# Attention with a Mish layer block on one core: the clamp of ten of 14 first-layer units moved from ScalarE to GpSimd, and GpSimd's work cut into more pieces

## The chip, the cores and the metric

The kernel runs on one core of a Trainium2 chip. The core has a matrix engine (TensorE; PE in the profile, with its weight loads as PEld), VectorE (DVE), ScalarE (ACT), GpSimd (POOL) and SyncE (SP), whose queue issues the DMAs. Each engine works through its own list of instructions in order and waits for the others by semaphores. The metric is the device time of one execution in microseconds, as the median of several runs. All times below are microseconds unless marked ns.

## The reference, cut to what matters

One transformer block in float32 on 2048 rows of 512: an adaptive layer norm, full softmax attention with 32 heads of 16, a gated residual, a second layer norm, and two dense layers (512 to 1792 to 512) with the Mish activation between them.

```python
h = _layernorm(x, axis=-1) * (1 + ca) + sa
x = x + ga * _A_ref(h, A_wqkv, A_wo)          # softmax(q k^T / 4) v, then wo
h = _layernorm(x, axis=-1) * (1 + cb) + sb
x = x + gb * _B_ref(h, B_w1, B_b1, B_w2)
...
def _B_ref(x, w1, b1, w2):
    h = jnp.einsum("bsd,df->bsf", x, w1) + b1
    sp = jnp.log1p(jnp.exp(-jnp.abs(h))) + jnp.where(h > 0, h, jnp.zeros_like(h))
    act = h * jnp.tanh(sp)
    return jnp.einsum("bsf,fd->bsd", act, w2)
```

The kernel uses another form of Mish: with e = exp(min(h, 10)) and u = e (e + 2), it is h u / (u + 2). One over (u + 2) is made as exp(-ln(u + 2)) on ScalarE and refined by one Newton step.

## The kernel before, in words

The rows are cut into four blocks of 512 queries (`NB`), the heads into eight groups of four (`G`); a pair of block and group is an iteration `n`, and an iteration has 16 steps, one for each chunk `kc` of 128 keys. `step(t)` writes out one step, and two half steps make a step (`h` counts half steps). In a step TensorE makes four score products for this iteration (`score`, line 505), each followed on ScalarE by an exponential out of PSUM (`pr`, line 508), four products for the row maxima of a later iteration (`max_tile`, line 468), each reduced by VectorE (line 470), and at the end the product of probabilities and values of two steps earlier (`pv`, line 523). The products of lines 468 and 505 go round a ring of six PSUM banks (`ring`), and a bank comes free when VectorE or ScalarE has read it.

Beside them TensorE is given parts of a queue of other units: projections and weight preparation at first, and from about a third of the time on the layer block of one block of 512 queries, three times (`block(qb, t0)`; the last block's is made in `tail()` after attention is through). Its order is written out by hand with `queue_up` and `queue_down`: an up unit `f` (0 to 13) makes 128 columns of the first layer, a down unit `(gi, i)` adds a group of up units into 128 rows of the second. The units' order is up 0 to 4; down (0,0), up 5, down (0,1), up 6, down (0,2), down (0,3), up 7, up 8; the same again with the next group and up 9 to 12; down (2,0), up 13, and the rest. So up 8 and up 12 follow another up unit directly, as do 1 to 4. A unit takes two or four steps of TensorE's spare slots, and when its last product is out, `fin(h)` is called, with `h` the half step that follows.

What an up unit does behind TensorE is `mish`, in stages that `fin` puts into later half steps with `at(h, f)`. `hooks[h]` is a list that `run_hooks(h)` runs in order, twice a step, and the position there decides where in each engine's list an instruction stands. The stages before:

- s1, at `h`: `hb` = product + bias (ScalarE, line 713; VectorE, line 711, where no maxima are left to make)
- s2, at `h + 1`: the clamp, `ee` = relu(10 - hb) (ScalarE, line 716)
- s2b, at `h + 2`: `ee` = exp(10 - ee), which is exp(min(hb, 10)) (ScalarE, line 719)
- s3, at `h + 3`: `ee` = (ee + 2) ee (VectorE, line 722), then `hb` = hb ee (GpSimd, line 723)
- s4, at `h + 4`: `rr` = ln(ee + 2) (ScalarE, line 726)
- s5, at `h + 6`: `rr` = exp(-rr) (ScalarE, line 729), then on GpSimd five operations in lines 735 to 739, the rounding of the result to `a_h` (line 93, `hi_copy`) and the rest `a_l` = hb - a_h (line 96, `lo_sub`)

A down unit ends with a copy of its bank by ScalarE (`yd`, line 864) and an addition by GpSimd (`y`, line 865). Each iteration ends with `evac(n)`: ScalarE copies the accumulated attention output out of PSUM (line 537), DMAs spread it and the row sums, and for each pair of groups `norm` multiplies by the reciprocals on GpSimd (`od`, line 566), rounds (line 93) and subtracts (line 96) at a half step set by line 570. The tiles `ee` and `rr` have two buffers, `hb` three, `qq` one.

In `tail()` the same stages run without attention, with `tail=True`; there VectorE does what GpSimd does in lines 723 and 735 to 739.

Of the kernel before, what the change touches and what calls it, by code (L numbers as in the profile page):

```python
# [18 lines left out]
def adaln_block(ctx: ExitStack, tc: tile.TileContext, x, wqkv, wo, w1, b1, w2, c, w_mod, out):  # L19
    nc = tc.nc  # L20
# [510 lines left out]
    def evac(n):  # L531
# [30 lines left out]
        if g % 2 == 1 or n == NIT - 2:  # L562
            r = slice(0, P if g % 2 else 64)

            def norm():
                nc.gpsimd.tensor_mul(od[r], od[r], rb[r])
                oh, ol = o_hl[qb]
                hi_copy("p", oh[r, g // 2, :], od[r])
                lo_sub("p", ol[r, g // 2, :], od[r], oh[r, g // 2, :])
            at(2 * t1 + (29 if g == 1 else 17 if hurry else 23), norm)  # L570
# [128 lines left out]
    def mish(f, acc, tail):  # L699
# [15 lines left out]
        def s2():  # L715
            nc.scalar.activation(ee, hb, AF.Relu, bias=hcap, scale=-1.0)

        def s2b():
            nc.scalar.activation(ee, ee, AF.Exp, bias=hcap, scale=-1.0)  # L719

        def s3():
            nc.vector.scalar_tensor_tensor(ee, ee, 2.0, ee, op0=ALU.add, op1=ALU.mult)  # L722
            (nc.vector if tail else nc.gpsimd).tensor_mul(hb, hb, ee)  # L723
# [4 lines left out]
        def s5():  # L728
# [5 lines left out]
            else:  # L734
                nc.gpsimd.tensor_scalar(ee, ee, 1.0, 2.0, op0=ALU.mult, op1=ALU.add)
                nc.gpsimd.tensor_mul(qq, ee, rr)  # L736
                nc.gpsimd.tensor_scalar(qq, qq, -1.0, 2.0, op0=ALU.mult, op1=ALU.add)
                nc.gpsimd.tensor_mul(rr, rr, qq)  # L738
                nc.gpsimd.tensor_mul(hb, hb, rr)
            hi_copy("v" if tail and f > FT - 4 else "p", a_h, hb)  # L740
            lo_sub("v" if tail and f > FT - 4 else "p", a_l, hb, a_h)

        return (a_h, a_l), (s1, s2, s2b, s3, s4, s5)
# [7 lines left out]
    HELD = 2  # L751
    state = [({}, {}, {}, {}) for _ in range(NB)]

    def block(qb, t0):
# [79 lines left out]
        def up_unit(f, tag):  # L834
# [3 lines left out]
            act[f], stages = mish(f, acc, False)  # L838

            def fin(h):  # L840
                stages[0](idle(h))
                for i, s in zip((1, 2, 3, 4, 6), stages[1:]):
                    at(h + i, s)
                done["a", f] = h + 6
# [44 lines left out]
        def queue_down(gi, i):  # L889
            queue(lambda l=groups[gi][-1]: done.get(("a", l), 4 * T) + 1, lambda tag: down_unit(gi, i, tag))  # L890
# [53 lines left out]
    def tail():  # L944
# [64 lines left out]
        for u in range(FT + LAG):  # L1009
# [7 lines left out]
            for d, ss in ((2, (4, 5)), (1, (2, 3)), (0, (0, 1))):  # L1017
                if 0 <= u - d < FT:
                    for q in ss:
                        stages[u - d][q]()  # L1020
# [301 lines left out]
```

## Time and profile before

| | us |
|---|---|
| median of three runs | 1742.61 |
| lowest and highest run | 1740.09, 1744.63 |
| profiled execution | 1738.89 |
| its span in the profile | 1737.1 |
| granted TensorE clock, mean share | 0.998 |

The three layer blocks lie between about 560 and 1625 of the span; from about 1570 on there are no maxima left to make, and attention ends at about 1625. How to read the lines: the page gives for each engine busy time, share of the span and number of instructions. A row of busy time in a stretch gives the stretch, its length, then for PE, PEld, DVE, ACT and POOL the busy time and number of instructions, the granted clock, the share of DMA time and GB/s. A row of a timeline gives start, duration, engine, source line, operation, output and input, and in brackets the idle time before it and what ended it. A row of a group ends with total busy time, mean ns of one, and idle time before.

### The profile page before, as it was taken

The page shows a single profiled execution, that of the slowest core. Times are in us where ns is not written, and L with a number is a line of the kernel's source. Part 1 is how long each engine was busy: PE and PEld are TensorE (multiplying, and loading weights), DVE is VectorE, ACT ScalarE, POOL GpSimd, SP SyncE. Part 2 cuts the span into 40 slices and gives each one's busy share as a digit, 9 for nine tenths or more (in the row PEclk, how much of TensorE's full clock was granted, in tenths as well). Part 3 has the DMA queues.
Part 4 walks back from the last instruction along what each step waited for, and adds up shares of the span by engine and source line. Part 5 has one row for each costly group of instructions (what it writes and reads, how often), then busy time and mean ns, then how long its engine had stood idle before and what let it go on. Part 6 is the DMA issues. An engine that isn't in the chain of part 4 may idle for free.

```text
span 1737.1 us, 33698 instructions
## 1 busy us (share of the span) xinstructions
PE 1702.3 (98%) x12396; PEld 963.9 (55%) x12396; DVE 1464.9 (84%) x2464; ACT 1349.4 (78%) x2581; POOL 729.0 (42%) x723
## 2 busy tenths in 40 slices
PE   7999999999999999999999999999999999999999
PEld 5755655555435555555555555555555555554587
DVE  6987888888898998989889898888898999892377
ACT  6257777777777898888877898888878988888474
POOL 5131124665303373444523374434423464444552
PEclk9999999999999999999999999999999999999999
DMA  7777467777762432524353533434252543423261
GB/s 251 187 254 189 114 172 202 234 235 223 218 184 52 136 96 77 136 77 121 89 137 87 162 97 88 139 90 124 71 156 73 152 102 103 115 79 130 85 230 61
DMA packets 113997, 240.08 MB, mean 138 GB/s; under 512 B 24048, under 2 KB 49648, under 8 KB 107784
## 3 DMA queue, kind: packets, MB, share of 16 engines
q1 hardware_dynamic: 113832, 237.92, 48.0%
q8 instruction: 98, 1.61, 0.4%
q14 instruction: 67, 0.55, 0.1%
HBM read 179.95 MB, written 51.44 MB: 133 GB/s over the span
## 4 chain that ended last, share of the span: by engine, by line
PE 80%; DMA 8%; DVE 4%; POOL 2%; ACT 2%; issue 2%; SPq 1%; POOLq 0%; ACTq 0%; DVEq 0%
PE bk L523 26%; PE ring L468 19%; PE ring L505 18%; PE bk L130 12%; PE ring L124 2%; DMA qscr<-ql 2%; DVE mx L470 2%; PE ring L1028 1%; DMA w1scr<-hl 1%; ACT pr L508 1%; PE bk L124 1%; DMA woscr<-hl 1%; DMA xt<-in_A_x 1%; DMA kscr<-ql 1%; DMA hl<-in_B_w 1%
## 5 line engine op out<-in xcount | busy, mean ns | idle before, releaser
L470 DVE TENSOR_REDUCE mx<-ring 128x1 f32<-128x512 f32 x2048 | 1274.0, 682 | 166.5 <-PE ring L468 134.7
L508 ACT ACTIVATE pr<-ring 128x512 f32<-128x512 f32 x2048 | 1083.3, 603 | 256.1 <-PE bk L130 161.4
L468 PE MATMUL ring<-ka,qa 64*128 64x512 f32 x2048 | 850.6, 429 | 0.9 <-DVE mx L470 0.4
L505 PE MATMUL ring<-qa,ka 64*128 64x512 f32 x2048 | 726.1, 398 | 7.0 <-ACT pr L508 5.8
L468 PEld LDWEIGHTS ring<-ka,qa 64*128 64x128 f32 x2048 | 366.4, 184 | 414.2 <-DVE mx L470 334.5
L523 PE MATMUL bk<-pr,vg 128*32 128x512 f32 x4096 | 546.3, 606 | 0.0
L505 PEld LDWEIGHTS ring<-qa,ka 64*128 64x128 f32 x2048 | 374.1, 185 | 88.3 <-ACT pr L508 34.4
L130 PE MATMUL bk<-h,w 64*128 64x512 f32 (+1 forms) x1080 | 279.0, 392 | 1.4 <-ACT pr L508 1.3
L130 PE MATMUL bk<-w,a_h 64*128 64x512 f32 x608 | 204.9, 416 | 1.4 <-ACT pr L508 1.2
L130 PEld LDWEIGHTS bk<-h,w 64*128 64x128 f32 x1080 | 178.5, 184 | 19.0 <-ACT pr L508 8.7
L723 POOL TENSOR_TENSOR hb<-hb,ee 128x512 f32<-128x512 f32 x42 | 54.0, 1286 | 293.9 <-DVE ee L722 293.9
L523 PEld LDWEIGHTS bk<-pr,vg 128*32 128x32 f32 x4096 | 81.6, 108 | 131.8 <-issue 126.0
L130 PE MATMUL bk<-w,a_l 64*128 64x512 f32 x304 | 119.4, 393 | 0.0
L130 PEld LDWEIGHTS bk<-w,a_h 64*128 64x128 f32 x608 | 100.9, 184 | 10.4 <-ACT pr L508 5.8
L865 POOL TENSOR_TENSOR y<-yd,y 128x512 f32<-128x512 f32 x48 | 62.0, 1295 | 80.4 <-ACT yd L864 80.2
L736 POOL TENSOR_TENSOR qq<-ee,rr 128x512 f32<-128x512 f32 x42 | 54.3, 1292 | 76.9 <-ACT rr L729 76.7
L130 PE MATMUL bk<-w,o_hl 64*128 64x512 f32 x288 | 81.5, 414 | 2.2 <-POOL o_hl L93 1.1
L96 POOL TENSOR_TENSOR a_l<-hb,a_h 128x512 fp32r<-128x512 f32 x53 | 72.3, 1363 | 4.4
L130 PEld LDWEIGHTS bk<-w,a_l 64*128 64x128 f32 x304 | 56.0, 184 | 3.0
L130 PE MATMUL bk<-h_h,wl 64*128 64x512 f32 x168 | 56.8, 419 | 0.0
L722 DVE SCALAR_TENSOR_TENSOR ee<-ee 128x512 f32<-128x512 f32 x56 | 41.4, 740 | 17.0 <-ACT ee L719 17.0
L738 POOL TENSOR_TENSOR rr<-rr,qq 128x512 f32<-128x512 f32 x42 | 54.1, 1287 | 3.5
(185 smaller groups left out, 1703.1 us busy)
## 6 DMA issues: line engine op xcount, KB each, us to landing
ka<-kscr SPq DMA_DIRECT2D x124, 384.0 KB
w<-w2scr SPq DMA_DIRECT2D x56, 512.0 KB
w<-w1scr SPq DMA_DIRECT2D x46, 512.0 KB
vg<-vscr SPq DMA_DIRECT2D x32, 552.0 KB
qa<-qscr SPq DMA_DIRECT2D x124, 100.0 KB
kscr<-qh SPq DMA_DIRECT2D x16, 512.0 KB
qscr<-qh SPq DMA_DIRECT2D x32, 256.0 KB
hl<-in_B_w SPq DMA_DIRECT2D x28, 256.0 KB
```

Of the source, the lines that this page charges most:

```text
L96: (nc.gpsimd if eng == "p" else nc.vector).tensor_sub(lo, src, hi.bitcast(F32))
L124: nc.tensor.matmul(acc, l, r, start=start, stop=stop)
L130: i = nc.tensor.matmul(acc, l[64 * g:64 * g + 64], r[64 * g:64 * g + 64], start=start and not g, stop=bool(stop and g))
L468: nc.tensor.matmul(pm, qt[64 * s:64 * s + 64, qs * P:(qs + 1) * P], kt[64 * s:64 * s + 64, kb * TB:(kb + 1) * TB], start=True, stop=True)
L470: nc.vector.tensor_reduce(out=mxs[n][:, s, 4 * j + qs, kb:kb + 1], in_=pm, op=ALU.max, axis=AX.X)
L505: nc.tensor.matmul(p_, kt[64 * s:64 * s + 64, kc * P:(kc + 1) * P], qt[64 * s:64 * s + 64, :], start=True, stop=True)
L508: e = nc.scalar.activation(pr, p_, AF.Exp, scale=SCALE)
L523: nc.tensor.matmul(accs[n][32 * h:32 * h + 32, :], vgs[n][:, o:o + 32], pts.pop((t, h)), start=(kc == 0), stop=(kc == 15))
L723: (nc.vector if tail else nc.gpsimd).tensor_mul(hb, hb, ee)
L736: nc.gpsimd.tensor_mul(qq, ee, rr)
L738: nc.gpsimd.tensor_mul(rr, rr, qq)
L865: nc.gpsimd.tensor_add(y[i], yd, y[i])
```

## The change

- The clamp of units 0 and 5 to 13 (`CLAMP_P`) is made on GpSimd, as `ee` = min(hb, 10) times 1; the exponential of these units then has neither scale nor bias. Units 1 to 4 and the tail keep ScalarE's.
- The clamp's stage (wherever it runs) is put at the head of the list of half step `h + 1`, ahead of what stands there already.
- GpSimd's share of a unit: the addition ee + 2 moves from s5 into s3 and writes `qq` in place of `ee`; s5 keeps two GpSimd operations at `h + 6`; the two products move to a stage s6 at `h + 8`, rounding and subtraction to s7 at `h + 9`.
- `done["a", f]` is `h + 8` in place of `h + 6`, and a down unit is ready at that half step in place of one later.
- `norm` is three functions at three half steps that follow each other; for the last group of a block (`hurry`) all three stay in one.
- In the tail s6 and s7 run together with s4 and s5, in the old order.

```diff
@@ -562,12 +562,11 @@
-            def norm():
-                nc.gpsimd.tensor_mul(od[r], od[r], rb[r])
-                oh, ol = o_hl[qb]
-                hi_copy("p", oh[r, g // 2, :], od[r])
-                lo_sub("p", ol[r, g // 2, :], od[r], oh[r, g // 2, :])
-            at(2 * t1 + (29 if g == 1 else 17 if hurry else 23), norm)
+            oh, ol = [v[r, g // 2, :] for v in o_hl[qb]]
+            norm = (lambda: nc.gpsimd.tensor_mul(od[r], od[r], rb[r]), lambda: hi_copy("p", oh, od[r]),
+                    lambda: lo_sub("p", ol, od[r], oh))
+            for i, f in enumerate(norm):
+                at(2 * t1 + (29 if g == 1 else 17 if hurry else 23) + (0 if hurry else i), f)
...
-    def mish(f, acc, tail):
+    def mish(f, acc, tail, clamp="a"):
...
         def s2():
-            nc.scalar.activation(ee, hb, AF.Relu, bias=hcap, scale=-1.0)
+            if clamp == "a":
+                nc.scalar.activation(ee, hb, AF.Relu, bias=hcap, scale=-1.0)
+            else:
+                nc.gpsimd.tensor_scalar(ee, hb, HCAP, 1.0, op0=ALU.min, op1=ALU.mult)
 
         def s2b():
-            nc.scalar.activation(ee, ee, AF.Exp, bias=hcap, scale=-1.0)
+            if clamp == "a":
+                nc.scalar.activation(ee, ee, AF.Exp, bias=hcap, scale=-1.0)
+            else:
+                nc.scalar.activation(ee, ee, AF.Exp)
 
         def s3():
             nc.vector.scalar_tensor_tensor(ee, ee, 2.0, ee, op0=ALU.add, op1=ALU.mult)
-            (nc.vector if tail else nc.gpsimd).tensor_mul(hb, hb, ee)
+            if tail:
+                nc.vector.tensor_mul(hb, hb, ee)
+            else:
+                nc.gpsimd.tensor_mul(hb, hb, ee)
+                nc.gpsimd.tensor_scalar(qq, ee, 1.0, 2.0, op0=ALU.mult, op1=ALU.add)
...
             else:
-                nc.gpsimd.tensor_scalar(ee, ee, 1.0, 2.0, op0=ALU.mult, op1=ALU.add)
-                nc.gpsimd.tensor_mul(qq, ee, rr)
+                nc.gpsimd.tensor_mul(qq, qq, rr)
                 nc.gpsimd.tensor_scalar(qq, qq, -1.0, 2.0, op0=ALU.mult, op1=ALU.add)
+
+        def s6():
+            if not tail:
                 nc.gpsimd.tensor_mul(rr, rr, qq)
                 nc.gpsimd.tensor_mul(hb, hb, rr)
+
+        def s7():
             hi_copy("v" if tail and f > FT - 4 else "p", a_h, hb)
             lo_sub("v" if tail and f > FT - 4 else "p", a_l, hb, a_h)
 
-        return (a_h, a_l), (s1, s2, s2b, s3, s4, s5)
+        return (a_h, a_l), (s1, s2, s2b, s3, s4, s5, s6, s7)
...
+    CLAMP_P = (0, 5, 6, 7, 8, 9, 10, 11, 12, 13)
...
-            act[f], stages = mish(f, acc, False)
+            act[f], stages = mish(f, acc, False, "p" if f in CLAMP_P else "a")
...
                 stages[0](idle(h))
-                for i, s in zip((1, 2, 3, 4, 6), stages[1:]):
+
+                hooks.setdefault(h + 1, []).insert(0, stages[1])
+                for i, s in zip((2, 3, 4, 6, 8, 9), stages[2:]):
                     at(h + i, s)
-                done["a", f] = h + 6
+                done["a", f] = h + 8
...
-            queue(lambda l=groups[gi][-1]: done.get(("a", l), 4 * T) + 1, lambda tag: down_unit(gi, i, tag))
+            queue(lambda l=groups[gi][-1]: done.get(("a", l), 4 * T), lambda tag: down_unit(gi, i, tag))
...
-            for d, ss in ((2, (4, 5)), (1, (2, 3)), (0, (0, 1))):
+            for d, ss in ((2, (4, 5, 6, 7)), (1, (2, 3)), (0, (0, 1))):
```

## The prediction, made before the changed kernel had run

> **What bounds the kernel now.** I read the page first (busy time, chain of waits), then the busy time of each engine in one long stretch, then single steps of the main loop, then the timelines of ScalarE and GpSimd around one first-layer unit.
>
> ```profile
> span 1737.1 us, 33698 instructions
> PE 1702.3 (98%) x12396; PEld 963.9 (55%) x12396; DVE 1464.9 (84%) x2464; ACT 1349.4 (78%) x2581; POOL 729.0 (42%) x723
> PE 80%; DMA 8%; DVE 4%; POOL 2%; ACT 2%; issue 2%; SPq 1%; POOLq 0%; ACTq 0%; DVEq 0%
> ...
> 575.00:1575.00 1000.00, 998.17 (x7560) 547.04 (x7554) 893.81 (x1521) 854.23 (x1649) 449.84 (x429) 1.00 0.40 107
> ```
>
> The last line is the stretch in which the second layer block runs beside attention: wall time, then busy time of PE, PEld, DVE, ACT, POOL. TensorE is busy all the time, yet a busy TensorE includes a matmul that is late. So the question is how long a step lasts. A step ends with the product of line 523, and I cut the stretch at its starts. These are the steps around unit 9 of the first of the three blocks; the order of the columns is the same.
>
> ```profile
> 753.79:756.74 2.95, 2.95 (x23) 1.76 (x23) 2.53 (x5) 2.74 (x7) 0.00 (x0) 1.00 0.66 223
> 756.74:759.80 3.06, 3.06 (x23) 1.80 (x22) 2.60 (x5) 3.06 (x8) 0.00 (x0) 1.00 0.49 180
> 759.80:762.64 2.84, 2.84 (x24) 1.52 (x23) 2.84 (x6) 2.68 (x7) 1.91 (x2) 1.00 0.02 8
> 762.64:765.48 2.84, 2.84 (x25) 1.53 (x23) 2.49 (x5) 2.58 (x7) 0.90 (x1) 1.00 0.01 3
> 765.48:768.32 2.84, 2.84 (x24) 1.69 (x22) 2.81 (x7) 2.57 (x7) 2.59 (x4) 1.00 0.00 0
> ```
>
> The floor is 2.84, TensorE's own. The first two steps are 0.11 and 0.22 longer, and in the second ScalarE is busy 3.06 of 3.06 while VectorE is busy 2.60. ScalarE's timeline says with what:
>
> ```profile
> 754.16 0.70 ACT L713 ACTIVATE hb<-bk,b1c 128x512 f32<-128x512 f32 x1
> 754.73 0.62 ACT L508 ACTIVATE pr<-ring 128x512 f32<-128x512 f32 x1
> 755.56 0.60 ACT L508 ACTIVATE pr<-ring 128x512 f32<-128x512 f32 x1 [0.21 <-PE ring L505]
> 756.05 0.72 ACT L716 ACTIVATE ee<-hb,hcap 128x512 f32<-128x512 f32 x1
> 756.67 1.56 ACT L508 ACTIVATE pr<-ring 128x512 f32<-128x512 f32 x3
> 758.10 0.74 ACT L719 ACTIVATE ee<-ee,hcap 128x512 f32<-128x512 f32 x1
> 758.71 2.08 ACT L508 ACTIVATE pr<-ring 128x512 f32<-128x512 f32 x4
> ...
> 760.62 0.78 ACT L726 ACTIVATE rr<-ee,two 128x512 f32<-128x512 f32 x1
> ...
> 763.50 0.64 ACT L729 ACTIVATE rr<-rr 128x512 f32<-128x512 f32 x1
> ...
> 765.86 0.60 ACT L864 COPY yd<-bk 128x512 f32<-128x512 f32 x1
> ```
>
> The three softmax exponentials at 756.67 take 758.10 - 756.67 = 1.43, so 0.48 each, start to start; the clamp of line 716 takes 756.67 - 756.05 = 0.62. A step has four exponentials, 4 x 0.48 = 1.92. With one more instruction of about 0.62 that is 2.54, under 2.84: the steps that hold only line 726, only 729 or only 864 last 2.84. With two more (713 and 716) it is 3.16, over by 0.32. ScalarE falls behind by that, the banks of the ring come free late, and TensorE pays 0.11 + 0.22 = 0.33 over two steps. So in a unit it is ScalarE's second extra instruction that sets the end, although ScalarE is idle elsewhere.
>
> **The change part by part.** The order of instructions on TensorE, VectorE and SP's queue (all DMAs) is as before, and ScalarE's differs by 30 clamps alone. Only GpSimd's is rearranged.
>
> *The clamp.* Ten of 14 units in three blocks: 30 instructions leave ScalarE and 30 join GpSimd. What each is worth:
>
> ```profile
> L716 ACT ACTIVATE ee<-hb,hcap 128x512 f32<-128x512 f32 x42 | 30.2, 720 | 0.0
> ...
> L735 POOL TENSOR_SCALAR ee<-ee x42: 617/618/623, 597.4 to 1619.8; 128x512 f32<-128x512 f32 x42
> ```
>
> Line 735 is a GpSimd tensor_scalar of the same shape and with two operations too, so I price the new one at its 0.62. In unit 9 the bias ends at 754.86, the clamp would run to about 755.57, and the exponential's turn comes at 758.10 - 0.62 = 757.48. GpSimd has nothing in that window (0.00 busy in the first two steps), so the wait the change adds to the exponential is hidden with 1.9 to spare. Without that cover the four softmax exponentials behind it wait as well, and TensorE with them.
>
> That holds for 22 of the 30 units: number 0, and those that follow a second-layer unit, where GpSimd is idle. Two units of the other blocks, and one with an evacuation:
>
> ```profile
> 1137.98:1140.92 2.94, 2.94 (x25) 1.75 (x24) 2.53 (x5) 2.74 (x6) 0.00 (x0) 1.00 0.71 249
> 1140.92:1143.97 3.05, 3.05 (x25) 1.79 (x24) 2.59 (x5) 3.05 (x8) 0.00 (x0) 1.00 0.30 123
> 1521.21:1524.15 2.94, 2.94 (x25) 1.76 (x24) 2.88 (x7) 2.74 (x7) 0.00 (x0) 1.00 0.50 178
> 1524.15:1527.21 3.06, 3.06 (x25) 1.49 (x24) 2.78 (x6) 3.06 (x8) 0.00 (x0) 1.00 0.02 5
> 783.11:786.42 3.31, 3.31 (x23) 1.56 (x23) 3.31 (x6) 3.16 (x8) 1.90 (x2) 1.00 0.49 134
> ...
> 784.24 0.59 ACT L537 COPY ot<-bk 128x512 f32<-128x512 f32 x1
> ```
>
> The excess over two floors is 2.94 + 3.05 - 5.68 = 0.31 and 2.94 + 3.06 - 5.68 = 0.32. I leave 0.02 to the bias and exponential that stay and take 0.30: 22 x 0.30 = 6.6 gained. Bounds: 22 x 0.11 = 2.4 if only the first step's part comes back, 22 x 0.33 = 7.3 if all does.
>
> In four of the 22 the next step also holds the copy of line 537, as at 783.11: 3.31, that is 0.47 over. Its own load is 1.92 + 0.48 + 0.62 = 3.02, or 0.18 over; the other 0.3 is the backlog that the clamp left. 4 x 0.3 = 1.2 gained, between 0 and 4 x 0.47 = 1.9.
>
> *The pairs.* Units 8 and 12 follow units 7 and 11 directly, five times in the stretch. There GpSimd still works on the unit before, and the new order is: last product of 7, clamp of 8, then rounding and subtraction of 7.
>
> ```profile
> 730.58 0.70 ACT L713 ACTIVATE hb<-bk,b1c 128x512 f32<-128x512 f32 x1
> 734.51 0.74 ACT L719 ACTIVATE ee<-ee,hcap 128x512 f32<-128x512 f32 x1
> ...
> 732.31 1.29 POOL L739 TENSOR_TENSOR hb<-hb,rr 128x512 f32<-128x512 f32 x1
> 733.69 0.62 POOL L93 TENSOR_SCALAR a_h<-hb 128x512 fp32r<-128x512 f32 x1
> 734.39 1.30 POOL L96 TENSOR_TENSOR a_l<-hb,a_h 128x512 fp32r<-128x512 f32 x1
> ...
> 735.93 0.68 DVE L722 SCALAR_TENSOR_TENSOR ee<-ee 128x512 f32<-128x512 f32 x1
> ```
>
> The clamp would take the slot at 733.69 and end at 734.31; the exponential's turn is 734.51 - 0.62 = 733.89. ScalarE then idles about 0.5, nearly what it saved, so the unit gains 0.1 at most there. The subtraction moves by 0.70 to 735.09 - 736.39 and lies across line 722, VectorE's two-operand instruction. What such a meeting costs, the trace has once:
>
> ```profile
> 641.67 1.29 POOL L566 TENSOR_TENSOR od<-od,rb 128x512 f32<-128x512 f32 x1
> ...
> 641.88 1.63 DVE L722 SCALAR_TENSOR_TENSOR ee<-ee 128x512 f32<-128x512 f32 x1
> ...
> 642.21:645.79 3.58, 3.36 (x24) 1.33 (x23) 3.58 (x5) 3.42 (x8) 3.41 (x4) 1.00 0.57 149
> ```
>
> Line 722 took 1.63 instead of 0.68, and the step, one with an evacuation, 3.58 instead of 3.31: 0.27 for 0.95 of delay, or 0.74 if the floor is the comparison. Here the delay would be 736.39 - 735.93 = 0.46 or a little more, so 0.13 to 0.36 a pair. Against 0.1 to 0.3 gained I take 0 for the five, from 1.5 gained to 5 x 0.74 = 3.7 lost.
>
> The Trainium skill, page "SBUF — State Buffer", section "Who interferes with whom", states that a VectorE instruction with two SBUF inputs and a GpSimd instruction that reads SBUF exclude each other, the later one waiting for the whole of the earlier. By that rule line 722 would start at 736.39 in every pair; the trace agrees (1.63 at 641.88, od's end at 642.96 plus 0.68 is 643.64, and it ended at 643.51).
>
> *Units 11 to 13 of the last block* run after the maxima are through, where ScalarE paces the steps.
>
> ```profile
> 1592.86 1.28 POOL L739 TENSOR_TENSOR hb<-hb,rr 128x512 f32<-128x512 f32 x1
> ...
> 1594.45 0.74 ACT L719 ACTIVATE ee<-ee,hcap 128x512 f32<-128x512 f32 x1
> ```
>
> Units 11 and 13 find GpSimd free and give 0.62 each. Unit 12's clamp comes behind the product at 1592.86, runs 1594.23 to 1594.85, and the exponential slips from 1594.45 to about 1594.9; the subtraction behind the clamp then delays line 722 too, some 0.7 in all. Sum: -0.62 - 0.62 + 0.7; I take 0.5 gained, from 1.9 gained to 1.0 lost.
>
> *The rest.* GpSimd's addition of two moves from behind the logarithm to ahead of it: same work, done while GpSimd waits anyway. The last four instructions of a unit now stand behind the y addition of the next second-layer unit, which waits for ScalarE's copy; the activations are needed at least four half steps later, and what is late then is only GpSimd's queue, which idles 55% of the stretch. The three pieces of the attention output get parted in three groups only: the piece of 1.29 at 641.67 goes ahead of the unit's end, and another subtraction of 1.29 comes to lie where it was, across the same line 722. Zero, within 0.5 either way.
>
> Sum: -6.6 - 1.2 + 0 - 0.5 + 0 = -8.3. The profiled execution took 1738.89 (its span 1737.1 and 1.8 around it), so 1730.6 on its own scale; it lies 3.7 under the median of the runs, 1742.61, and the forecast for a median is 1742.6 - 8.3 = 1734.3.
>
> **The rivals.**
> - *VectorE's line 722 makes the second long step.* It starts near the end of that step and would keep the 0.22:
>
> ```profile
> 759.47 0.68 DVE L722 SCALAR_TENSOR_TENSOR ee<-ee 128x512 f32<-128x512 f32 x1
> ```
>
>   For it: VectorE's queue is full from there on. Against: VectorE is busy 2.60 of 3.06 in the long step and 2.84 of 2.84 in the next, which is not longer for it. If it holds, only 22 x 0.11 = 2.4 and the 0.5 come: 1739.7.
> - *GpSimd gives part back at the pairs.* The meeting with line 722 costs the full 0.74 in all five and unit 12 of the last block its 1.0: -8.3 + 3.7 + 1.5 = -3.1, so 1739.5. For it: the order of the pair above. Against: in the one case of the trace 0.95 of delay cost 0.27.
> - *GpSimd becomes ScalarE's pacer*, the slower side. If the three output pieces (1.29 + 0.62 + 1.29 = 3.2) or a unit's tail stand ahead of a clamp, it ends 3.2 - 1.9 = 1.3 past the exponential's turn, 0.7 worse than now; in all 27 units of the stretch 27 x 0.7 = 19 lost, 1761. It decides from 1.9 + 0.62 = 2.5 of GpSimd work ahead of the clamp. Against: GpSimd's idle time in these steps.
> - *The exponential gains too.* It loses its bias operand; the exponential of line 729 without one takes 0.64 where line 719 takes 0.74. With all upper bounds: 7.3 + 1.9 + 1.5 + 1.9 = 12.6, so 1730.0.
>
> **How the numbers follow.** Forecast 0.62, line 722 0.13, pairs 0.12, GpSimd as pacer 0.08, the larger gain 0.05. About 0.3% (5.2) is what a measurement of this kernel can tell from no change. Under 1737.4 lie 0.57 of the forecast's 0.62, the larger gain and 0.01 of the rest: 0.63 faster. Same: 0.05 + 0.12 + 0.12 = 0.29. Slower: 0.08. The bounds add to -7.3 - 1.9 - 1.5 - 1.9 - 0.5 = -13.1 and -2.4 + 3.7 + 1.0 + 0.5 = +2.8; the range leaves the outermost of both: 1729.5 to 1743.5.
>
> **What would show it.** Right: in the units after a second-layer unit the two steps behind the bias last 2.84 to 2.87, ScalarE does not wait before the exponential, and GpSimd's clamp starts about 0.1 after the bias. Steps with 537 and 726 fall to about 3.0. In units 8 and 12 ScalarE waits up to 0.5 for GpSimd and line 722 takes more than 1. Wrong: a second step that stays at 3.06 (then it was VectorE), waits of ScalarE for GpSimd in other units, or TensorE waiting for a rounded activation.

## The result, and the profile after

| | us |
|---|---|
| changed kernel, median of 14 runs | 1745.38 (1740.68 to 1747.36) |
| kernel before, median of 14 runs beside them | 1740.44 (1735.66 to 1744.63) |
| ratio, 95% interval | 1.0025 (1.0017 to 1.0034) |
| profiled execution of the changed kernel | 1744.71 |
| its span in the profile, granted clock | 1742.9, 0.996 |

The forecast was 1734.3 with 1729.5 to 1743.5. The kernel became slower by 0.25%, and a ratio of 1 lies outside the interval: a forecast of 8 saved turned into some 5 lost. One execution in the experiments was disturbed, at 3078.92 in experiment 1: it is counted in the median of 1735.78 there (1734.96 without it) and in no ratio.

Line numbers from here on are those of the changed kernel: bias 712 (VectorE's 710), ScalarE's clamp 716, GpSimd's clamp 718, the exponential 722 (after ScalarE's clamp) or 724 (after GpSimd's), VectorE's two-operand instruction 727 (722 before), GpSimd's products 731, 744, 749, 750. First the page's line of busy times:

```profile
PE 1704.7 (98%) x12396; PEld 961.9 (55%) x12396; DVE 1463.2 (84%) x2464; ACT 1336.3 (77%) x2551; POOL 788.9 (45%) x753
```

The view of one source line, the clamp: lowest, median and highest duration in ns, start of the first and the last, and below who waited for it, how long in all and how often.

```profile
L718 POOL TENSOR_SCALAR ee<-hb x30: 1920/1921/1934, 589.1 to 1617.9; 128x512 f32<-128x512 f32 x30
...
  ACT ee L724: 9.6, 6
```

GpSimd is busy 788.9 - 729.0 = 59.9 more, which is 30 x 1.92 and little else. I had priced the clamp at 0.62. It takes three times as long in all 30 places, and in six units the exponential waits for it, 9.6 in all. Which steps these are is seen in the busy time by steps of the changed kernel: the first two steps of unit 9 of the first block, the third of unit 10 (with the copy of line 537), the second and third of unit 7, the second of unit 8, and the second and third of unit 12 of the last block.

```profile
753.71:756.65 2.94, 2.94 (x23) 1.76 (x22) 2.53 (x5) 2.73 (x7) 1.78 (x1) 1.00 0.76 208
756.65:759.55 2.90, 2.90 (x23) 1.58 (x23) 2.44 (x5) 2.59 (x6) 0.14 (x1) 1.00 0.61 213
782.72:786.03 3.31, 3.30 (x24) 1.56 (x23) 3.31 (x6) 3.17 (x8) 1.89 (x2) 1.00 0.58 150
719.98:723.09 3.11, 3.11 (x25) 1.55 (x24) 2.84 (x7) 2.60 (x6) 2.86 (x4) 1.00 0.00 0
723.09:726.38 3.29, 3.29 (x24) 1.32 (x22) 3.29 (x6) 3.14 (x7) 2.35 (x3) 1.00 0.02 5
732.23:736.15 3.92, 3.29 (x23) 1.59 (x22) 3.22 (x6) 2.58 (x6) 3.67 (x4) 1.00 1.01 184
1594.70:1597.36 2.66, 2.66 (x20) 1.20 (x19) 0.00 (x0) 1.02 (x3) 2.58 (x2) 1.00 0.00 0
1597.36:1603.13 5.77, 3.56 (x20) 1.84 (x19) 0.85 (x2) 4.87 (x9) 4.69 (x5) 0.82 0.14 17
```

The kernel before, in four steps that answer to these (unit 7's third, unit 8's second, and the second and third of the last block's unit 12):

```profile
724.38:727.37 2.99, 2.99 (x25) 1.41 (x23) 2.99 (x6) 2.83 (x7) 1.91 (x2) 1.00 0.02 5
733.20:736.22 3.02, 3.02 (x24) 1.60 (x23) 2.52 (x5) 3.02 (x7) 2.31 (x3) 1.00 1.05 227
1592.95:1596.22 3.27, 2.66 (x19) 1.21 (x19) 0.93 (x1) 3.27 (x8) 3.10 (x3) 1.00 0.00 0
1596.22:1598.94 2.72, 2.63 (x19) 1.29 (x18) 0.72 (x2) 2.64 (x7) 1.91 (x3) 1.00 0.03 3
```

Three things are to be seen. In an isolated unit the first step stays at 2.94, the second falls from 3.06 to 2.90, and the evacuation's step stays at 3.31. In the second step of the five pairs, 3.92 to 4.18 long, TensorE is busy 3.3: it waits, which it did not before. And in unit 12 of the last block the second step falls from 3.27 to 2.66, as in units 11 and 13, but the third, in which the late exponential now stands, grows from 2.72 to 5.77.

I cut both traces at the starts of line 523, counted the steps through, and added, unit by unit, the first four steps from the bias on. Changed minus before: 22 isolated units -2.1, the five pairs +5.0 (0.90 to 1.17 each, all in the second step), units 1 to 4 -0.0, the last block's units 11 to 13 -0.62, +3.0 and -0.53. In unit 12 the granted clock is 0.82 in the step of 5.77 and 0.80 in the next, which is 3.21 long and was 2.68; by my estimate up to 0.18 x 5.77 = 1.0 and 0.5 of the loss are this dip. Whether it belongs to the stall is not shown: the clock dips without one too, in both traces to 0.83 between 520 and 530. The sum is +4.7, against 4.9 between the medians and 5.8 between the two profiled executions; 1.7 of these lie behind the last block's units, where the changed kernel's clock dips once more, and ahead of the first unit the changed kernel is 1.0 earlier.

The pair in the timelines of the changed kernel, ScalarE and GpSimd (start, duration, line; in brackets the idle time and what ended it):

```profile
729.60 0.70 ACT L712 ACTIVATE hb<-bk,b1c 128x512 f32<-128x512 f32 x1
...
730.99 2.24 ACT L508 ACTIVATE pr<-ring 128x512 f32<-128x512 f32 x4 [0.20 <-PE ring L505]
734.56 0.63 ACT L724 ACTIVATE ee<-ee 128x512 f32<-128x512 f32 x1 [1.33 <-POOL ee L718]
...
731.23 1.29 POOL L750 TENSOR_TENSOR hb<-hb,rr 128x512 f32<-128x512 f32 x1
732.61 1.92 POOL L718 TENSOR_SCALAR ee<-hb 128x512 f32<-128x512 f32 x1
734.61 0.62 POOL L93 TENSOR_SCALAR a_h<-hb 128x512 fp32r<-128x512 f32 x1
735.31 1.75 POOL L96 TENSOR_TENSOR a_l<-hb,a_h 128x512 fp32r<-128x512 f32 x1
```

The order is the forecast's (product of unit 7, clamp of unit 8, rounding, subtraction). With 0.62 the clamp would have ended at 733.23, when ScalarE's exponentials of the softmax run out (730.99 + 2.24 = 733.23). It ends at 734.53, ScalarE stands still for 1.33, and the four exponentials behind line 724 with it: no bank of the ring comes free, and TensorE waits (0.63 ahead of the product of line 468 at 735.73, ended by line 508).

### The profile page after: what moved, and what is told of

The parts are those of the page before. It is cut to its first block, busy times and chain, and to the rows that moved or that the text cites. A ratio compares the mean times of both kernels' runs of the same rounds, so it can differ in the third digit from the quotient of the medians.

```text
span 1742.9 us, 33720 instructions
## 1 busy us (share of the span) xinstructions
PE 1704.7 (98%) x12396; PEld 961.9 (55%) x12396; DVE 1463.2 (84%) x2464; ACT 1336.3 (77%) x2551; POOL 788.9 (45%) x753
## 4 chain that ended last, share of the span: by engine, by line
PE 83%; DMA 6%; DVE 5%; ACT 2%; POOL 2%; issue 2%; SPq 1%; ACTq 0%; POOLq 0%; DVEq 0%
PE bk L523 27%; PE ring L468 20%; PE ring L505 18%; PE bk L130 11%; PE ring L124 3%; DVE mx L470 2%; ACT pr L508 2%; PE ring L1044 1%; PE bk L124 1%; DMA qscr<-ql 1%; DMA w2scr<-hl 1%; DMA xt<-in_A_x 1%; DMA kscr<-ql 1%; DMA rb<-rscr 0%; DMA y<-in_A_x 0%
## 5 line engine op out<-in xcount | busy, mean ns | idle before, releaser
L718 POOL TENSOR_SCALAR ee<-hb 128x512 f32<-128x512 f32 x30 | 57.7, 1922 | 167.0 <-ACT hb L712 155.8
L744 POOL TENSOR_TENSOR qq<-qq,rr 128x512 f32<-128x512 f32 x42 | 54.3, 1294 | 80.4 <-ACT rr L738 80.4
```

The lines of the kernel that those rows point to most:

```text
L718: nc.gpsimd.tensor_scalar(ee, hb, HCAP, 1.0, op0=ALU.min, op1=ALU.mult)
L744: nc.gpsimd.tensor_mul(qq, qq, rr)
```

## The experiments

Each kernel's medians stand beside runs of the kernel before from the same chip. Steps are cut as above, and sums over units are made in the same way.

**1. The clamp's instruction exchanged for one of the form that I had taken the price from.** The clamp is left out in the ten units; GpSimd multiplies by 0.5 and adds 0 in its place.

```diff
-                nc.gpsimd.tensor_scalar(ee, hb, HCAP, 1.0, op0=ALU.min, op1=ALU.mult)
+                nc.gpsimd.tensor_scalar(ee, hb, 0.5, 0.0, op0=ALU.mult, op1=ALU.add)
```

> The changed kernel with the ten units' GpSimd instruction doing hb times 0.5 plus 0 in place of min(hb, 10) times 1: the clamp is left out and these units' exponential gets half the argument; same instructions, same places. Theory A (the price of min: 1.92 in the changed kernel's profile where I had taken 0.62): the instruction takes 0.62, the second step of the pairs 8 and 12 falls from 3.92 to 4.18 to about 3.0, and ScalarE no longer waits for GpSimd; 5 x 1.0 at the pairs, some 2.4 at unit 12 of the last block and 2 x 0.5 behind units 7 and 11 of the first come back, 8.4 in all, so a ratio to before of about 0.998. Theory B (the place in GpSimd's queue, whatever the instruction costs): the pairs' second step stays over 3.7 and the ratio at 1.002.

Measured: median 1735.78 against 1741.98, ratio 0.9966 (0.9952 to 0.9979). Nothing but the operation differs from the changed kernel, and the loss of 0.25% becomes a gain of 0.34%: 0.0059 x 1741 = 10.3 come back, where I had expected 8.4. For its steps the kernel was profiled once more:

> The same kernel as in the first experiment (hb times 0.5 plus 0 in place of the minimum, so the clamp is left out in ten units), for a profile of an ordinary execution. If the price of the minimum is all that is wrong at the pairs: the second step behind units 8 and 12 lasts 2.83 to 3.0 where the changed kernel had 3.92 to 4.18, no wait of ScalarE's exponential for GpSimd over 0.5, and the step of 5.77 at unit 12 of the last block is under 3.6. If the place in the queue counts too, ScalarE still waits there, by 0.3 to 0.5.

The view of line 718 there, and then the busy time in the second step of unit 8:

```profile
L718 POOL TENSOR_SCALAR ee<-hb x30: 609/620/625, 591.2 to 1611.9; 128x512 f32<-128x512 f32 x30
```

```profile
733.99:736.83 2.84, 2.84 (x24) 1.55 (x23) 2.32 (x5) 2.71 (x6) 2.76 (x4) 1.00 1.10 231
```

3.92 became 2.84. The five pairs together gain 0.3 on the kernel before where the changed kernel lost 5.0. The isolated units gain 2.7, hardly more than the 2.1 of the changed kernel, so for them the length of the clamp matters little.

**2. The price list.** One operation of GpSimd in each of the units, all from `hb` to `ee` in the same shape (what follows in the unit computes something else; written here one to a line, with its line number behind).

```diff
+                if f == 0:   g.tensor_scalar(ee, hb, HCAP, 1.0, op0=ALU.min, op1=ALU.mult)          # L720
+                elif f == 5: g.tensor_scalar(ee, hb, 1.0, HCAP, op0=ALU.mult, op1=ALU.min)          # L722
+                elif f == 6: g.tensor_scalar(ee, hb, 0.5, -HCAP, op0=ALU.mult, op1=ALU.max)         # L724
+                elif f == 7: g.tensor_scalar(ee, hb, HCAP, -50.0, op0=ALU.min, op1=ALU.max)         # L726
+                elif f == 9: g.tensor_scalar(ee, hb, 0.0, 0.5, op0=ALU.subtract, op1=ALU.mult)      # L728
+                elif f == 10: g.tensor_scalar_min(ee, hb, HCAP)                                     # L730
+                elif f == 11: g.tensor_scalar(ee, hb, nhalf, 0.0, op0=ALU.mult, op1=ALU.add)        # L732
+                elif f == 13: g.tensor_scalar(ee, hb, hcap, 1.0, op0=ALU.min, op1=ALU.mult)         # L734
+                else: g.tensor_scalar(ee, hb, 0.5, 0.0, op0=ALU.mult, op1=ALU.add)                  # L736
```

> The changed kernel with another GpSimd instruction in each unit in place of min(hb, 10) times 1; the units that do not clamp get half the argument or minus half of it. What one takes, by theory A1 (a minimum or maximum is slow, wherever it stands) and A2 (any immediate form but multiply-add is slow) and A3 (an operand from a tile is what is slow): min then mult 1.92 in all; mult then min 1.92, 1.92, 0.62; mult then max 1.92, 1.92, 0.62; min then max 1.9 to 3.2, 1.92, 0.62; subtract then mult 0.62, 1.92, 0.62; min alone 1.92 or a little under, 1.92, 0.62; mult by a column of a tile, then add 0.62, 0.62, 1.9; min with a column of a tile, then mult 1.92, 1.92, 1.9 or more.

The groups by line (busy time, mean ns of one):

```profile
L734 POOL TENSOR_SCALAR ee<-hb,hcap 128x512 f32<-128x512 f32 x3 | 6.0, 1994 | 15.8 <-ACT hb L712 11.2 <-DVE hb L710 4.6
L728 POOL TENSOR_SCALAR ee<-hb 128x512 f32<-128x512 f32 x3 | 5.8, 1936 | 16.7 <-ACT hb L712 16.7
L722 POOL TENSOR_SCALAR ee<-hb 128x512 f32<-128x512 f32 x3 | 5.8, 1930 | 16.6 <-ACT hb L712 16.6
L720 POOL TENSOR_SCALAR ee<-hb 128x512 f32<-128x512 f32 x3 | 5.8, 1926 | 35.5 <-ACT hb L712 35.5
L730 POOL TENSOR_SCALAR ee<-hb 128x512 f32<-128x512 f32 x3 | 4.5, 1502 | 16.9 <-ACT hb L712 16.9
L736 POOL TENSOR_SCALAR ee<-hb 128x512 f32<-128x512 f32 x6 | 3.7, 613 | 0.0
L732 POOL TENSOR_SCALAR ee<-hb,nhalf 128x512 f32<-128x512 f32 x3 | 2.1, 688 | 23.7 <-ACT hb L712 17.5 <-DVE hb L710 6.2
L726 POOL TENSOR_SCALAR ee<-hb 128x512 f32<-128x512 f32 x3 | 1.8, 613 | 24.7 <-ACT hb L712 24.7
```

It is not the comparison as such: min followed by max takes 0.613, as multiply followed by add does, while min with a multiplication takes 1.93 in either order, subtraction with a multiplication 1.94, and min alone 1.50. So none of the three theories holds: min, max at 0.613 speaks against A1 and A2, the column operand at 0.688 against A3. Some pairs of operations are fast and others are not; why these is not shown by any run here. The Trainium skill, page "GPSIMD Engine Reference", section "Engine selection", calls GpSimd's operations with one input roughly line-rate. 0.61 goes with that, beside the 0.68 that VectorE's reduction of line 470 takes for as many elements; 1.50 and 1.93 do not: the measurement decides, and it depends on the pair of operations.

**3. The change without its pairs.** Units 8 and 12 keep ScalarE's clamp.

```diff
-    CLAMP_P = (0, 5, 6, 7, 8, 9, 10, 11, 12, 13)
+    CLAMP_P = (0, 5, 6, 7, 9, 10, 11, 13)
```

> The changed kernel with units 8 and 12 taken out of the list, so that these six keep ScalarE's clamp; all else stays. If the loss sits at the units that follow another unit directly, as the steps of the changed kernel say (5.0 in five pairs and 3.0 at unit 12 of the last block), the time falls by about 8 from the changed kernel's 1745.4, to a ratio of about 0.998 to before. If the loss is spread (the instruction disturbs VectorE or TensorE in the other 24 units too), it falls by 6/30 of the loss at most and the ratio stays over 1.001.

Measured: median 1738.31, ratio 0.9979 (0.9969 to 0.999). Against the changed kernel's 1.0025 this is 0.0046 x 1741 = 8.0, and it comes from six of 30 units: 5.0 in the pairs, the rest from the last block's unit 12, whose steps are again as before. The isolated units give 1.9 with a clamp of 1.92.

**4. The pieces alone.** No unit is clamped on GpSimd; GpSimd's order is the changed kernel's.

```diff
-    CLAMP_P = (0, 5, 6, 7, 8, 9, 10, 11, 12, 13)
+    CLAMP_P = ()
```

> The changed kernel with an empty list of units: every clamp stays on ScalarE, and what is left of the change is GpSimd's share in five pieces, the output in three, and the clamp at the head of its half step. If the pieces cost nothing, as I priced them: ratio 1.000 within 0.001, and the two steps behind a bias stay at 2.94 and 3.06. If the pieces are what made the kernel slower: ratio about 1.0025 and steps of 3.5 where the output's pieces meet line 727.

Measured: median 1740.82, ratio 0.9996 (0.9987 to 1.0005), isolated units +0.1, pairs 0.0. One step gains: the meeting at 641.88 stays, but its like in the last block (unit 3) falls from 3.55 to 3.31. The five pieces and the three half steps cost nothing.

**5. The relief alone.** In the kernel before, the clamp of the ten units is left out (exponential of half the argument), and GpSimd gets nothing.

```diff
-            nc.scalar.activation(ee, hb, AF.Relu, bias=hcap, scale=-1.0)
+            if tail or f in (1, 2, 3, 4):
+                nc.scalar.activation(ee, hb, AF.Relu, bias=hcap, scale=-1.0)
...
+            else:
+                nc.scalar.activation(ee, hb, AF.Exp, scale=0.5)
```

> The kernel before with the clamp of the ten units left out altogether (their exponential reads hb with scale 0.5), nothing added to GpSimd and nothing moved: what ScalarE's relief is worth by itself. My prediction's theory (all of the 0.33 over the floor is ScalarE's backlog): the two steps behind the bias fall to 2.84 to 2.87, and 22 x 0.30 and 1.2 more come, ratio about 0.995. The changed kernel's steps say instead that only 0.17 of the second step is the relief: 2.94 and 2.90, the steps with an evacuation stay at 3.31, units 8 and 12 gain 0.17 each and the last block's three some 1.5, in all about 6, ratio 0.9965. If GpSimd's instruction costs something in the units without a neighbour, the second step falls under the 2.90 that the changed kernel has there.

Measured: median 1733.30 against 1740.65, ratio 0.996 (0.9946 to 0.9974). This is all that the move could bring. The steps: unit 9's second step, the evacuation's step of unit 10, two steps of unit 9 of the second block, and the second step of unit 7.

```profile
756.48:759.32 2.84, 2.84 (x24) 1.52 (x23) 2.38 (x5) 2.59 (x6) 0.00 (x0) 1.00 0.70 230
782.70:786.00 3.30, 3.30 (x26) 1.58 (x22) 3.30 (x7) 3.16 (x7) 1.90 (x2) 1.00 0.49 133
1138.84:1141.68 2.84, 2.84 (x23) 1.53 (x23) 2.39 (x5) 2.59 (x6) 0.00 (x0) 1.00 0.41 166
1141.68:1144.98 3.30, 3.15 (x25) 1.47 (x23) 3.27 (x8) 3.13 (x7) 1.91 (x2) 1.00 0.00 0
...
721.26:724.33 3.07, 3.07 (x24) 1.50 (x23) 2.79 (x6) 2.59 (x6) 0.00 (x0) 1.00 0.00 0
```

The second step falls to the floor, the first stays at 2.94, and the evacuation's step does not move. In the second block's unit 9 the 0.22 won in one step is lost in the next: 3.30, where the kernel before had 3.09; VectorE is busy 3.27 of it. Three units are like it. In unit 7 the second step itself stays at 3.07, with ScalarE busy only 2.59 of it: something else set it all along; four units are like that. In all seven the row maxima of an iteration end in these steps, but not the same engine is the limit. In the first three it is VectorE, where line 479's two reductions meet its own two-operand instruction (line 726 in this kernel). In the other four VectorE is busy 2.79 of 3.07, and what the step has more is a product of TensorE: the transposition of the maxima in line 485, once an iteration. The kernel before shows it in a step without any bias, clamp or exponential of a unit (busy time, and TensorE's timeline):

```profile
768.32:771.38 3.06, 3.06 (x25) 1.51 (x23) 2.87 (x6) 2.08 (x5) 2.89 (x4) 1.00 0.02 5
...
769.32 0.28 PE L485 MATMUL ring<-ident,mm 128*32 128x128 f32 x1
769.53 0.50 PE L468 MATMUL ring<-ka,qa 64*128 64x512 f32 x1
```

The next product starts 0.21 behind line 485's, and the step is 0.22 over 2.84 with no other engine full; all 21 steps with line 485 between 560 and 1570 last 3.05 or more. So the floor of these steps is TensorE's own, some 3.06. The seven units gain nothing, and the other 15 gain 3.4 together, 0.23 each.

**6. The clamp of units 8 and 12 half a step earlier**, ahead of the last two products of the unit before, with the price of 1.92 unchanged.

```diff
-                hooks.setdefault(h + 1, []).insert(0, stages[1])
+                hooks.setdefault(h if f in (8, 12) else h + 1, []).insert(0, stages[1])
```

> The changed kernel with the clamp of units 8 and 12 one half step earlier in GpSimd's list, ahead of the last two products of the unit before. If the 1.0 a pair is ScalarE's wait for a clamp that starts late: the clamp starts right behind the bias and ends at 1.92 + 0.1, before the exponential's turn at about 2.6 behind the bias' end, the second step falls to 2.9 to 3.2, and the time by 5 to 7 from the changed kernel's (ratio about 0.999). Against it stands what is late next: the activations of units 7 and 11 come 1.9 later, and TensorE may wait for a_l by up to 0.5, which would show as a wait of line 130 for line 96; or line 727 meets the products instead, and the step stays over 3.4.

Measured: median 1734.67, ratio 0.9969 (0.9956 to 0.9981): faster than both kernels, and nothing of the computation is left out. The timelines of GpSimd and ScalarE in unit 8, and the busy time in its second step:

```profile
730.87 1.92 POOL L718 TENSOR_SCALAR ee<-hb 128x512 f32<-128x512 f32 x1 [0.60 <-ACT hb L712]
...
733.59 0.63 ACT L724 ACTIVATE ee<-ee 128x512 f32<-128x512 f32 x1
```

```profile
732.72:735.54 2.82, 2.82 (x23) 1.54 (x22) 2.31 (x5) 2.57 (x6) 2.65 (x3) 1.00 1.04 218
```

The same slow clamp no longer delays the exponential once it stands ahead of the two products, the first of which now starts at 732.88. So price and place decide together: two products and 1.92 behind the bias was too much, 1.92 is not. Against the changed kernel 0.0056 x 1741 = 9.7 come back, more than the 5 to 7 that I had expected, as unit 12 of the last block loses nothing either. The five pairs gain 0.2 together, where leaving the clamp out gains 1.0 (experiment 5): in three of them the next step lasts 3.15 or 3.16 in place of 2.84.

**7. The first step.** As experiment 3, with the bias left out: `hb` is a plain copy out of PSUM.

```diff
-                nc.scalar.activation(hb, acc, AF.Identity, bias=b1c[:, f:f + 1])
+                nc.scalar.copy(hb, acc)
```

> The kernel without the pairs, with the bias left out: hb is a plain copy out of PSUM in all units but the tail's. It tells what the first long step is. Theory C (TensorE's next unit waits for its bank until hb has read it, line 712 takes 0.70 where the copy of a second-layer unit takes 0.59 and costs 0.01): the first step falls from 2.94 to 2.85, the second stays at 2.90, and 38 units give about 0.09 each, so 3.4 less than the kernel without the pairs, ratio about 0.996. Theory D (ScalarE's load in that step): the copy saves 0.09 of a load that is under the floor anyway, nothing changes.

Measured: median 1734.58, ratio 0.9967 (0.9955 to 0.998). The copy, which takes 0.58 where the bias took 0.70, in ScalarE's timeline, TensorE's first weight load for the next unit, and the busy time in unit 9's first step; in the last line, the same weight load in the kernel before:

```profile
752.46 0.58 ACT L715 COPY hb<-bk 128x512 f32<-128x512 f32 x1
753.10 0.18 PEld L130 LDWEIGHTS bk<-w,a_h 64*128 64x128 f32 x1
```

```profile
752.07:754.92 2.85, 2.85 (x24) 1.68 (x23) 2.44 (x5) 2.57 (x7) 1.79 (x1) 1.00 0.63 196
```

```profile
754.91 0.18 PEld L130 LDWEIGHTS bk<-w,a_h 64*128 64x128 f32 x1
```

The first step falls by 0.09 for 0.12 of ScalarE's time; taking the clamp away, 0.62 to 0.72, had left it at 2.94. The first step's excess is the bank that the next unit's products of line 130 wait for until `hb` has been read out of it: the weight load starts 0.06 behind the copy's end (753.04) here and 0.05 behind the bias's end (754.86) before. That holds where the clamp is gone. In units 1 to 4, 8 and 12, which keep ScalarE's clamp here, the second step takes back what the first gave (in unit 1 of the first block 2.93 and 3.06 before, 2.84 and 3.17 here): there ScalarE's load sets the two steps together. So against experiment 3 some 0.0012 x 1741 = 2.1 come, and not the 3.4 of theory C.

**8. The fast pair of operations in the change's own place.** A lower bound of -50 under an exponential.

```diff
-                nc.gpsimd.tensor_scalar(ee, hb, HCAP, 1.0, op0=ALU.min, op1=ALU.mult)
+                nc.gpsimd.tensor_scalar(ee, hb, HCAP, -50.0, op0=ALU.min, op1=ALU.max)
```

> The changed kernel with one operation of the clamp exchanged: min with 10 and then max with -50 in place of min with 10 and then a multiplication by 1 (a lower bound of -50 under an exponential changes nothing that is seen). In the run of prices the pair min, max took 0.613 where min, multiply took 1.926. Theory A (the price of the clamp alone turns the gain into a loss): line 718 takes 0.61, the second step of units 8 and 12 lasts 2.83 in place of 3.92 to 4.18, unit 12 of the last block 3.4 in place of 5.77, and the two steps of units 7 and 11 of the first block lose their +0.35; ratio to the kernel before 0.996 to 0.998. Theory B (the place of the clamp on GpSimd, not its length, is what costs): the pairs stay at +0.3 or more each and the ratio at 0.999 or more.

Measured: median 1736.64 against 1739.57, ratio 0.9977 (0.9964 to 0.999). Line 718 takes 0.61, and units 7 and 11 of the first block lose their extra. The busy time in two steps of unit 8 of the second block, and from the timelines the two instructions that meet in them:

```profile
1118.57:1121.44 2.87, 2.87 (x24) 1.58 (x23) 2.34 (x5) 2.59 (x7) 2.62 (x4) 1.00 0.17 37
1121.44:1124.78 3.34, 3.34 (x24) 1.41 (x23) 3.34 (x6) 3.26 (x7) 2.32 (x3) 1.00 0.85 196
```

```profile
1120.60 1.29 POOL L96 TENSOR_TENSOR a_l<-hb,a_h 128x512 fp32r<-128x512 f32 x1
...
1121.30 1.13 DVE L727 SCALAR_TENSOR_TENSOR ee<-ee 128x512 f32<-128x512 f32 x1
```

The second step is 2.87, so theory A holds for it. What I had not written down is the third, 2.84 before: the subtraction now lies across line 727, which takes 1.13 in place of 0.68, and VectorE sets 3.34. All five pairs together +0.4. In unit 12 of the last block the third step, 5.77 in the changed kernel, is 3.54, still more than the 2.72 before: ScalarE waits 0.89 for the clamp there, since a step without maxima leaves less time. By the Trainium skill, page "SBUF — State Buffer", section "Who interferes with whom", line 727 would wait for the whole of the subtraction and end at 1121.89 + 0.68 = 1122.57; it ended at 1122.43, so the trace agrees within 0.14.

**9. All 14 units**, with min and max.

```diff
-    CLAMP_P = (0, 5, 6, 7, 8, 9, 10, 11, 12, 13)
+    CLAMP_P = tuple(range(FT))
```

> As the min, max kernel, with the clamp on GpSimd in all 14 units, units 1 to 4 (beside evacuation and the pieces of the attention output) too. If ScalarE's backlog sets their steps as in the other units, each of the 12 gains up to 0.2, 2.4 together, and the ratio falls by 0.001 to about 0.995 to 0.997. If their steps of 3.31 are set by the evacuation (as in the kernel with pieces alone, where nothing moved) nothing changes against the min, max kernel, and the clamp can only be late behind the pieces: the wait of line 724 on line 718 shows in units 1 to 4, with up to +0.3 each.

Measured: median 1741.07, ratio 1.0006 (0.9995 to 1.0017). Units 1 to 4 lose 4.2, more than the 3.1 that the other ten gain. Unit 4 of the first block in the timelines of GpSimd and ScalarE, and the busy time in its second step:

```profile
641.13 1.29 POOL L566 TENSOR_TENSOR od<-od,rb 128x512 f32<-128x512 f32 x1
...
645.82 0.61 POOL L718 TENSOR_SCALAR ee<-hb 128x512 f32<-128x512 f32 x1
...
646.46 0.63 ACT L724 ACTIVATE ee<-ee 128x512 f32<-128x512 f32 x1 [1.95 <-POOL ee L718]
```

```profile
643.52:648.06 4.54, 3.31 (x23) 1.58 (x23) 3.22 (x5) 2.59 (x6) 4.30 (x5) 1.00 0.98 168
```

The clamp comes behind an attention output piece, a rounding and two products (641.13 to 645.73), and even at 0.61 it is late by 1.95. The wait was foreseen, but not its size: up to 1.3 a unit, not 0.3.

**10. What is left of the second step.** The clamp is left out, the changed kernel's pieces and order are kept.

```diff
-                nc.gpsimd.tensor_scalar(ee, hb, HCAP, 1.0, op0=ALU.min, op1=ALU.mult)
+                pass
...
-                nc.scalar.activation(ee, ee, AF.Exp)
+                nc.scalar.activation(ee, hb, AF.Exp, scale=0.5)
```

> The clamp is left out in the ten units (exponential of half the argument, no GpSimd instruction in its place), the pieces and the order of the changed kernel are kept. The second step of the 22 units was 3.06 before, 2.90 with the change (with the clamp at 1.92 and at 0.62 alike), 2.84 where the clamp was left out of the kernel before. If the remaining 0.06 comes from the GpSimd instruction or the wait on it, the second step is 2.84 here; if from the order of GpSimd's other work, it stays 2.90.

Measured: one run, 1732.17. Unit 9's second step is 2.83, so the remaining 0.06 does not come from the pieces.

**11. VectorE in GpSimd's place**, all 14 units, min alone.

```diff
-                nc.gpsimd.tensor_scalar(ee, hb, HCAP, 1.0, op0=ALU.min, op1=ALU.mult)
+                nc.vector.tensor_scalar_min(ee, hb, HCAP)
```

> The clamp on VectorE (min alone) in all 14 units, in place of GpSimd. VectorE has four reductions of 0.683 in a step of 2.84, so 0.11 is free in it, and a clamp of about 0.69 (the time of its other instructions of this shape) makes the second step VectorE's: 2.73 + 0.69 = 3.42, or 3.2 by its 2.53 to 2.60 of that step before. If so the second steps last 3.2 to 3.4 in place of 3.06, and the kernel is slower than before by 42 x 0.15 to 0.35 = 6 to 15 us. If the backlog is carried to the next step as ScalarE's is, the sum of the two counts in the same way. A rival: VectorE's reductions wait for products, so the clamp falls into its idle time and the second step is 2.84 to 2.90: 6 to 8 faster.

Measured: one run, 1737.52. The view of the clamp's line, and the busy time in the second step of unit 9:

```profile
L718 DVE TENSOR_SCALAR ee<-hb x42: 416/420/1418, 590.0 to 1610.6; 128x512 f32<-128x512 f32 x42
```

```profile
755.69:758.58 2.89, 2.89 (x23) 1.59 (x22) 2.77 (x6) 2.58 (x6) 0.00 (x0) 1.00 0.63 220
```

Here the rival was right for the isolated units: VectorE does it in 0.42, not 0.69, and the step is 2.89 as with GpSimd. The pairs (+0.5) and units 1 to 4 (+3.0) lose, where GpSimd is at work and the clamp takes up to 1.42. The 0.06 above the floor in the second step appears with the clamp on either engine (2.89, 2.90) and not where it is left out. The traces show where it sits: the first softmax exponential behind the unit's own, first in the changed kernel, then in experiment 5, in the second step of unit 9.

```profile
758.48 1.58 ACT L508 ACTIVATE pr<-ring 128x512 f32<-128x512 f32 x3 [0.31 <-PE bk L130]
```

```profile
758.24 1.57 ACT L508 ACTIVATE pr<-ring 128x512 f32<-128x512 f32 x3 [0.25 <-PE bk L130]
```

Both wait for a product of TensorE, and the idle time is 0.06 longer in the changed kernel. There ScalarE's queue holds a semaphore instruction more ahead of this exponential; in all, the view of line 508 counts 648 of them, against 544 in the kernel before and 554 in experiments 5 and 10, and 672 in this one. No run takes these instructions out and keeps the clamp, so that they are the cause is not shown.

## Why the prediction was wrong

*The step that failed first: the price of the clamp.* "Line 735 is a GpSimd tensor_scalar of the same shape and with two operations too, so I price the new one at its 0.62." The shape was the same, but the operations were multiply and add there and are min and multiply here: 1.92. The trace of before held no min on GpSimd at all, so the price was unknown and should have had bounds from both sides; I gave it none. The upper one stood in that trace, and I overlooked it: GpSimd's tensor_scalars of 0.62 there are all multiply and add, while line 107, a subtraction and a multiplication with two columns of scalars in the same shape, takes 2.08.

```profile
L107 POOL TENSOR_SCALAR xn<-y,ln_mv,ln_rs 128x512 f32<-128x512 f32 x12 | 25.0, 2080 | 1.3
```

Experiment 1 (the operation alone exchanged, 1.0025 to 0.9966), the price list and experiment 8 (0.9977) show that the price is what failed. The range was too narrow besides: its working adds up to +2.8, so 1745.4, but its upper end was put at 1743.5, while the lower end kept its whole sum; the 4.9 lost lies beyond the +2.8 as well.

*What the price did to the pairs* (forecast 0, bounds -1.5 to +3.7). The working was right in its order and its times: the clamp in the slot behind the product at 732.61, the exponential's turn when the softmax's run out. 1.92 - 0.62 = 1.3 is just the 1.33 that ScalarE waits. +5.0 in place of 0, outside the bounds, as these had held only the meeting with line 722 and not a later clamp. The same in unit 12 of the last block, where I had 0.7 lost against 0.62 gained and four steps grew by 3.0 together (by the estimate above up to 1.5 of it at a lower clock). These six instructions lost more than the other 24 gained.

*The term of 0.30 in the isolated units* (-6.6) was mis-sized, and would have been at the right price. I read both excesses, 0.11 and 0.22, as ScalarE's backlog, which the clamp's leaving would take away. Experiment 7 shows that a second limit stands behind it: with the clamp gone 0.11 stays, the handover of a bank, and goes with the end of the bias. Experiment 5 bounds the rest at 0.23 in 15 units and at 0 in seven, those at the end of an iteration's row maxima, where TensorE's line 485 (four units) or VectorE (three) is the limit; so the most was 3.4. The changed kernel got 2.1: 0.06 in each second step was not won back, in which ScalarE's list, that I took to differ by 30 clamps alone, also holds more semaphore instructions; and units 7 and 11 of the first block lost 0.36 each. There the long clamp pushes line 566 and what follows it back (720.20 and on) until a subtraction meets line 727, whose step is 3.29 in place of 2.99.

*The evacuation's steps* (-1.2): 0. They stay at 3.31 also with the clamp left out. VectorE is busy 3.31 of 3.31 there; the row that I had quoted, 3.31 of VectorE beside 3.16 of ScalarE, said so, and I took ScalarE's sum instead.

*The rest* (0 within 0.5): held, by experiment 4. Units 11 and 13 of the last block: -0.62 and -0.53, as forecast.

*The rivals.* "GpSimd becomes ScalarE's pacer" is what came, with its mechanism: the tail of a unit stands ahead of the clamp. Its point of decision was 2.5 of GpSimd work ahead of a clamp of 0.62; in the pair there are 2.2 (from the bias's end at 730.30 to 732.52), and the 1.3 that the clamp is longer make it 3.5. I had given it 0.08, and against it GpSimd's idle time in these steps, a mean over units that holds for 22 of them and not for five pairs. It was also written for "all 27 units", while it takes hold in six. That VectorE's line 722 makes the second long step falls for the units it was argued on: with the clamp left out that step is 2.84. It does take part in three others, in the step behind, where that line meets the two reductions of line 479 (VectorE busy 3.27 of 3.30 in experiment 5). A meeting of line 727 with a subtraction does come in the pairs (1.13 in experiment 8), once the price is right.

With the terms that the runs gave, at 0.61: isolated units -2.7, pairs +0.4, last block -0.6 + 0.2 - 0.5 = -0.9, together -3.2; measured in experiment 8 0.0023 x 1740 = 4.0. Of the 8.3 that I forecast, more than half would have been missing even at the price that I took.

## What to carry to other kernels

An engine's price for an operation is read from the same operation, not from the same shape: where the trace has none, measure it alone, or carry both ends of what the engine shows in that shape (here 0.62 and 2.08) through the sum. A move to an idle engine is judged at the few places where that engine is not idle, since one late instruction there stops everything that is queued behind its reader; moving these places (experiment 6) or taking them out (experiment 3) turned a loss of 0.25% into gains of 0.31% and 0.21%. And where two engines are both near full in a step, relieving one brings only the distance to the other.

## What the runs showed of the hardware that was not expected

- GpSimd, 128x512 in float32, one input: min, max 0.61 and multiply, add 0.61; min, multiply 1.93 in either order; subtract, multiply 1.94; min alone 1.50, slower than min with max.
- VectorE does min alone in 0.42 where its reduction of the same size takes 0.68, and in up to 1.42 beside a busy GpSimd.
- The operand of a column instead of a constant costs GpSimd some 0.07 (0.688 against 0.613, 1.994 against 1.926).
